# Query weights turned in 32x32 blocks on VectorE and gathered through DRAM, in place of transposing matmuls on TensorE

## The chip, the cores and the metric

The kernel runs on one core of a Trainium2 chip. The metric is the time of one execution on the device in microseconds (us), as the median of several runs. The engines of the core are named as the profile names them: PE is TensorE (PEld its weight loads), DVE is VectorE, ACT is ScalarE, POOL is GpSimd, and SP is SyncE, which issues all DMAs of this kernel.

## The reference

Attention by way of 49 agents, followed by a two-layer network with a squared ReLU, all in float32:

```python
B, N, C = (4, 12480, 128);  n_agents = 49;  d_ff = 2048

def sm(a, b):
    s = scale * (a @ b.transpose(0, 2, 1))
    s = s - s.max(-1, keepdims=True)
    e = np.exp(s)
    return e / (e.sum(-1, keepdims=True) + 1e-09)
a2k = sm(agents, k)            # 49 x N weights a batch
agent_v = a2k @ v              # 49 x 128
q2a = sm(q, agents)            # N x 49 weights: the "query weights"
x = (q2a @ agent_v)            # N x 128
h = np.maximum(x @ w_in, 0.0)
out = h * h @ w_out
```

## The kernel before

**Tiling.** The 49,920 tokens are cut into 52 groups of 960 (`BLK`, 13 groups a batch). A group is 8 tiles of 120 tokens (`TP` = 120, `NT` = 8) and is worked on in two halves of 480 tokens (`G`). The hidden dimension of 2048 is 16 chunks of 128; two chunks of one half make a *slot*, so a group has 16 slots (`SLOTS`), and slots are handled in pairs.

**What the main loop computes.** `w_in` is multiplied beforehand with the agents' values, once a batch (`tables`). A half's hidden values are then one product of its query weights, 49 rows and 480 columns, with that table. To keep float32 accuracy on the faster matmul type both operands are split into a rounded part (`hi`) and a remainder (`lo`), so that the product has three parts: hi with hi, hi with lo and lo with hi. Their rows stand on top of one another along the contraction: 49 rows of hi and 49 of lo, 98 (`K2`), then 30 more rows of hi (`SP` = 128 - 98) in the same tile `w`, and the 19 that are left over (`NL`) in a small tile `x`, which holds four copies of them, at partitions 0, 32, 64 and 96. `first(k)` (L341) issues four matmuls with `w` and four with `x` for a pair of slots; `hidden(k)` (L359) makes relu and square on ACT and DVE, and the split of the square on ACT, DVE and POOL; `second(k)` (L384) issues the 12 matmuls of the output a pair of slots, four slots behind. All of them pass `queued` (L334), so that their instructions bear line L337.

**How the query weights are made.** `queries(g + 1)` (L282) is a generator that advances by one step in slot 0 and in each slot from 2 on of group `g` (L492 to L496). The steps before:

1. load `qt`, the queries as 128 x 960 (L285);
2. 8 score matmuls into the bank `psa`, tokens on partitions (L290; each is two instructions in the trace);
3. maximum and subtraction on DVE (L293, L295);
4. exponential on ACT (L297);
5. sum and reciprocal on DVE (L300 to L302), product on POOL (L303);
6. the rounded half on ACT (L188) into tile `pp`, 98 columns a token;
7. the remainder on POOL (L190);
8. for each half: 4 matmuls with a unit matrix that turn `pp` (98 rows out, L312), a copy from `psa` to `w` on ACT (L317), and in the next step one DMA of the 30 rows (L320) and four of the 19 rows (L322).

The weights of a group must be in `w` and `x` when `first` of its first slot (or of its ninth, for the second half) runs.

**Other work beside it.** While a batch is in its main loop, `background(b + 1)` (L401) works through keys and values of the next batch in small steps: loads `kt` and `vt` (480 KB each, two buffers), score matmuls (L155), sums over the values (L235), the next tables (L266 to L277). It is spread over 88% of a batch's slots, and the last batch has none. `bank()` gives background and queries the same single PSUM bank `psa`; only before the main loop (`alone`) do they take banks of the pool `h`, of which there are three pairs. The hidden values use these three, and `o` is one bank.

**What sets the order.** Instructions are emitted in the order of the Python code; a planner at build time lays out each engine's order by that priority and by when it reckons an instruction's inputs to be ready, so that later emitted work can stand ahead where an engine would be free. On the chip each engine, SP with its DMAs too, goes through its own list in order and waits at the head for what it needs.

The prologue runs the first batch's keys and values (`whole_values`), `queries(0)` and `tables(0)`, and decodes `w_in` and `w_out`.

Of the kernel before, what the change touches and what calls it, by code (L numbers as in the profile page):

```python
# [9 lines left out]
F32 = mybir.dt.float32  # L10
F32R = mybir.dt.float32r
# [6 lines left out]
P = 128  # L18
TP = 120
NT = 8  # L20
BLK = TP * NT
G = BLK // 2
# [15 lines left out]
@with_exitstack  # L38
def agent_attention_relu2(ctx: ExitStack, tc: tile.TileContext, qT, kT, v, agT, w_in, w_out, outT):
    nc = tc.nc  # L40
    C, NTOK = qT.shape
    _, B, NA = agT.shape
    N = NTOK // B
    FF = w_in.shape[1]
    NCH = FF // P
    NB = N // BLK
    NTT = N // TP
    K2 = 2 * NA
    SP = P - K2
    NL = NA - SP  # L50
    NQ = P // 32
    scale = 1.0 / math.sqrt(C)

    const = ctx.enter_context(tc.tile_pool(name="const", bufs=1))
    kv = ctx.enter_context(tc.tile_pool(name="kv", bufs=2))
    sp = ctx.enter_context(tc.tile_pool(name="sp", bufs=NB))
    small = ctx.enter_context(tc.tile_pool(name="small", bufs=1))
    aw = ctx.enter_context(tc.tile_pool(name="aw", bufs=2))
    qp = ctx.enter_context(tc.tile_pool(name="qp", bufs=2))
    dec = ctx.enter_context(tc.tile_pool(name="dec", bufs=2))  # L60
    ps_h = ctx.enter_context(tc.tile_pool(name="ps_h", bufs=3, space=PSUM))
    ps_o = ctx.enter_context(tc.tile_pool(name="ps_o", bufs=1, space=PSUM))
    ps_a = ctx.enter_context(tc.tile_pool(name="ps_a", bufs=1, space=PSUM))

    ag = const.tile([C, B, NA], F32, name="ag")
# [2 lines left out]
    nc.gpsimd.memset(ones, 1.0)  # L68
    ident = const.tile([P, P], F32, name="ident")
    make_identity(nc, ident)  # L70
    identr = const.tile([TP, TP], F32R, name="identr")
    nc.scalar.copy(identr, ident[:TP, :TP])

    quad = const.tile([K2, 2, NA], F32, name="quad")
    nc.gpsimd.tensor_copy(quad, ident[:K2, :K2].rearrange("p (h a) -> p h a", h=2))
# [50 lines left out]
    last = {}  # L126
# [3 lines left out]
    def bank():  # L130
        if alone[0]:
            return ps_h.tile([P, 2, 512], F32, name="h")[:, 0, :]
        return ps_a.tile([P, 512], F32, name="psa")
# [51 lines left out]
    def halves(out, x, n, eng):  # L185

        w = x.shape[2]
        nc.scalar.copy(out[:, :, :w], x)  # L188
        yield
        last[eng] = eng.tensor_sub(out[:, :, n : n + w], x, out[:, :, :w].bitcast(F32))  # L190

    def whole_values(b, i, vt):
        st = state[b]
        e = st["s"][i]
        nc.vector.tensor_sub(e, e, st["mb"].rearrange("p (o a) -> p o a", o=1).broadcast_to([TP, NT, NA]))
        nc.scalar.activation(e, e, AF.Exp, scale=scale)
        if i == 0:
            st["pv"] = bank()
        for t in range(NT):
            nc.tensor.matmul(  # L200
                st["pv"][:NA, :C], e[:, t, :], vt[:, t, :], start=(i == 0 and t == 0), stop=(i == NB - 1 and t == NT - 1)
            )
        if i == 1:
            st["es"] = small.tile([TP, NT, NA], F32, name="es")
        if i > 0:
            nc.gpsimd.tensor_add(st["es"], st["es"] if i > 1 else st["s"][0], e)

# [35 lines left out]
    def tables(b):  # L243
        st = state[b]
        qd = quad.rearrange("p h a -> p (h a)")
        if "x" not in st:
            st["x"] = small.tile([K2, C + 1], F32, name="x")
            nc.vector.tensor_add(st["x"], st["av"][:, : C + 1], st["av"][:, C + 1 :])
        x = st["x"]
        yield  # L250
        pa = bank()
        nc.tensor.matmul(pa[:C, :K2], x[:, :C], qd, start=True, stop=True)
        nc.tensor.matmul(pa[:K2, K2 : K2 + 1], qd, x[:, C:], start=True, stop=True)
        yield
        av = small.tile([C, K2], F32, name="avT")
        nc.scalar.copy(av, pa[:C, :K2])
        rl = small.tile([K2, 1], F32, name="rl")
        nc.vector.tensor_scalar_add(rl, pa[:K2, K2 : K2 + 1], 1e-9)
        nc.vector.reciprocal(rl, rl)
        hi = st["hi"] = aw.tile([P, FF], F32R, name="aw_hi")  # L260
        ex = st["lo"] = aw.tile([P, NCH // NQ, P], F32R, name="aw_ex")
        for n in range(FF // 512):
            yield
            cs = slice(n * 512, (n + 1) * 512)
            pw = bank()
            nc.tensor.matmul(pw[:K2, :], av, win[:, cs], start=True, stop=True)  # L266
            yield
            last[nc.scalar] = nc.scalar.activation(hi[:K2, cs], pw[:K2, :], AF.Copy, scale=rl)
            lo = aw.tile([NA, 512], F32R, name="aw_lo", bufs=3)
            last[nc.vector] = nc.vector.scalar_tensor_tensor(  # L270
                out=lo, in0=pw[:NA, :], scalar=rl[:NA, :], in1=hi[:NA, cs].bitcast(F32),
                op0=ALU.mult, op1=ALU.subtract,
            )
            yield
            nc.sync.dma_start(hi[K2:, cs].bitcast(F32), lo[:SP, :].bitcast(F32))
            for t in range(NQ):
                nc.sync.dma_start(ex[t * 32 : t * 32 + NL, n, :].bitcast(F32), lo[SP:, t * P : (t + 1) * P].bitcast(F32))  # L277


    weights = {}  # L280

    def queries(g):  # L282
        b = g // NB
        qt = qp.tile([C, BLK], F32, name="qt", bufs=1)
        nc.sync.dma_start(qt, qT[:, g * BLK : (g + 1) * BLK])  # L285
        yield
        ps = bank()
        sv = ps[:TP, : NT * NA].rearrange("p (t a) -> p t a", a=NA)
        for t in range(NT):
            nc.tensor.matmul(sv[:, t, :], qt[:, t * TP : (t + 1) * TP], ag[:, b, :], start=True, stop=True)  # L290
        yield
        m = qp.tile([TP, NT, 1], F32, name="m", bufs=1)
        nc.vector.reduce_max(m, sv, axis=AX.X)  # L293
        e = qp.tile([TP, NT, NA], F32, name="e", bufs=1)
        nc.vector.tensor_sub(e, sv, m.broadcast_to([TP, NT, NA]))  # L295
        yield
        nc.scalar.activation(e, e, AF.Exp, scale=scale)  # L297
        yield
        z = qp.tile([TP, NT, 1], F32, name="z", bufs=1)
        nc.vector.reduce_sum(z, e, axis=AX.X)  # L300
        nc.vector.tensor_scalar_add(z, z, 1e-9)  # L301
        nc.vector.reciprocal(z, z)  # L302
        nc.gpsimd.tensor_mul(e, e, z.broadcast_to([TP, NT, NA]))  # L303
        yield
        pp = qp.tile([TP, NT, K2], F32R, name="pp", bufs=1)
        yield from halves(pp, e, NA, nc.gpsimd)
        weights[g] = []
        for j in range(2):
            yield
            pt = bank()  # L310
            for t in range(NT // 2):
                nc.tensor.matmul(  # L312
                    pt[:K2, t * TP : (t + 1) * TP], pp[:, j * (NT // 2) + t, :], identr, start=True, stop=True
                )
            w = qp.tile([P, G], F32R, name=f"w{j}", bufs=2)
            x = qp.tile([P, G], F32R, name=f"x{j}", bufs=2)
            nc.scalar.copy(w[:K2, :], pt[:K2, :G])  # L317
            weights[g].append((w, x))
            yield
            nc.sync.dma_start(w[K2:, :].bitcast(F32), w[:SP, :].bitcast(F32))  # L320
            for t in range(NQ):
                nc.sync.dma_start(x[t * 32 : t * 32 + NL, :].bitcast(F32), w[SP:NA, :].bitcast(F32))  # L322

    NP = NCH // 2
# [74 lines left out]
    def background(b):  # L401

        kt = load_keys(b, 0, kv, "kt")
        for i in range(NB):
            nxt = load_keys(b, i + 1, kv, "kt") if i + 1 < NB else load_values(b, 0, kv, "vt")
            yield from scores(b, i, kt)
            yield
            kt = nxt
        yield from maxima(b)
        yield  # L410
        vt = kt
        for i in range(NB):
            nxt = load_values(b, i + 1, kv, "vt") if i + 1 < NB else None
            yield from values(b, i, vt, nc.gpsimd)
            yield
            vt = nxt
        yield from tables(b)
# [64 lines left out]
    for k in range(total + LAG):  # L482
        if k < total:
            g, c = divmod(k, SLOTS)
            b, i = divmod(g, NB)
            if i == 0 and c == 0 and b + 1 < B:
                todo = background(b + 1)
                done = 0
            goal = (i * SLOTS + c + 1) * STEPS / (SPREAD * NB * SLOTS)
            while done < goal and step(todo):  # L490
                done += 1
            if c == 0 and g + 1 < B * NB:  # L492
                ahead = queries(g + 1)
                step(ahead)
            if c >= 2:
                step(ahead)  # L496
        if k % 2 == 0:
            hs = first(k) if k < total else ()
            if hs:
                hidden(k, hs[0])  # L500
            for n in range(2):
                if k + n >= LAG:
                    second(k + n - LAG)
            copied_out()
            if hs:
                hidden(k + 1, hs[1])
# [31 lines left out]
```

## Time and profile before

| | |
|---|---|
| median of 3 runs | 2060.38 us (2060.13 to 2062.12) |
| the profiled execution: its time | 2060.99 us |
| its span, first to last instruction | 2059.2 us |
| granted TensorE clock, mean | 0.992 |
| busy: PE, ACT, DVE, POOL | 99%, 87%, 82%, 62% |
| DMA: moved, share of 16 engines | 131.36 MB, 21.0% |

The profiled execution is one run on the chip; its rows carry the name of the tile written, an arrow, and the tiles read, with the line of the kernel behind the engine. A busy share is an average over stages. [...] Of a DMA the profile shows its issue on SP; when its data moves is seen in the DMA share and GB/s of short windows.

### The profile page before, as it was taken

How to read it: one execution, taken by the hardware profiler on the slowest of the kernel's cores; microseconds unless marked ns; L12 is line 12 of the kernel's file. 1: busy time of each engine (PE TensorE's matmuls, PEld its weight loads, DVE VectorE, ACT ScalarE, POOL GpSimd, SP SyncE). 2: the span in 40 equal slices, each digit the busy share in tenths (PEclk: the TensorE clock that was granted, in tenths of full speed). 3: DMA queues.
4: the chain of work that ended last, by engine and by line, in shares of the span. 5: the costliest groups of instructions: out<-in, count | busy, mean ns of one | idle time of the engine just before them, and what ended most of it. 6: DMA issues, size and time to landing. Idle time of an engine off the chain costs nothing.

```text
span 2059.2 us, 31857 instructions
## 1 busy us (share of the span) xinstructions
PE 2029.8 (99%) x11014; PEld 1589.8 (77%) x11014; DVE 1686.1 (82%) x1842; ACT 1782.3 (87%) x2100; POOL 1279.2 (62%) x1104
## 2 busy tenths in 40 slices
PE   9799999999999999999999999999999999999999
PEld 8588777777788777777778877777777777777777
DVE  5687888888887888888887788888888888888887
ACT  3478999989888899989888899998889898989897
POOL 3555787765544587776555467877555555656555
PEclk9799999999999999999999999999999999999999
DMA  9532122121122221221112212211111111111100
GB/s 288 160 92 76 59 72 74 53 77 41 45 81 65 62 72 54 72 71 57 55 54 69 68 42 61 74 58 49 42 50 36 45 36 46 37 41 36 38 23 20
DMA packets 55604, 131.36 MB, mean 64 GB/s; under 512 B 6660, under 2 KB 34388, under 8 KB 55444
## 3 DMA queue, kind: packets, MB, share of 16 engines
q1 hardware_dynamic: 55444, 129.33, 21.0%
q8 instruction: 88, 1.44, 0.3%
q14 instruction: 72, 0.59, 0.1%
HBM read 80.97 MB, written 25.56 MB: 52 GB/s over the span
## 4 chain that ended last, share of the span: by engine, by line
PE 53%; DVE 1%; issue 0%; ACT 0%
PE o L337 33%; PE h L337 16%; PE psa L290 2%; PE psa L155 1%; PE psa L312 1%; PE psa L235 1%; PE psa L266 0%; DVE h L337 0%; DVE gg L337 0%; DVE g_lo L337 0%; DVE z L301 0%; ACT r L337 0%; DVE ob L337 0%; ACT g_hi L337 0%; DVE av L241 0%
## 5 line engine op out<-in xcount | busy, mean ns | idle before, releaser
L372 POOL TENSOR_TENSOR g_lo<-gg,g_hi 128x480 fp32r<-128x480 f32 x832 | 999.2, 1222 | 685.7 <-DVE gg L337 489.1
L337 ACT ACTIVATE r<-h 128x960 f32<-128x960 f32 x832 | 800.9, 963 | 150.0 <-PE h L337 141.9
L337 ACT ACTIVATE g_hi<-r 128x960 fp32r<-128x960 f32 x832 | 837.7, 1007 | 34.1 <-POOL e L190 0.7
L337 DVE TENSOR_TENSOR h<-r,h 128x960 f32<-128x960 f32 x416 | 482.4, 1160 | 160.2 <-ACT r L337 157.8
L337 DVE TENSOR_TENSOR gg<-r,h 128x960 f32<-128x960 f32 x416 | 477.8, 1149 | 81.9 <-ACT r L337 81.0
L337 PE MATMUL o<-g_hi,wo_hi 128*128 128x480 f32 x1664 | 543.0, 408 | 0.0
L337 DVE TENSOR_TENSOR g_lo<-h,g_hi 128x960 fp32r<-128x960 f32 x416 | 480.8, 1156 | 45.2 <-ACT g_hi L337 8.1
L337 PE MATMUL o<-g_hi,wo_lo 128*128 128x480 f32 x1664 | 498.7, 381 | 0.0
L337 PE MATMUL o<-g_lo,wo_hi 128*128 128x480 f32 x1664 | 497.7, 380 | 0.0
L337 PE MATMUL h<-w,aw_hi 128*128 128x480 f32 x1664 | 483.3, 398 | 9.7 <-DVE gg L337 8.1
L337 PEld LDWEIGHTS o<-g_hi,wo_hi 128*128 128x128 f32 x1664 | 280.8, 188 | 118.8 <-issue 70.1
L337 PEld LDWEIGHTS o<-g_hi,wo_lo 128*128 128x128 f32 x1664 | 313.4, 188 | 51.3
L337 PEld LDWEIGHTS o<-g_lo,wo_hi 128*128 128x128 f32 x1664 | 313.0, 188 | 50.9
L337 PEld LDWEIGHTS h<-w,aw_hi 128*128 128x128 f32 x1664 | 289.0, 190 | 56.9 <-DVE gg L337 17.5
L337 PE MATMUL h<-x,aw_ex 19*128 19x480 f32 x1664 | 205.4, 481 | 0.1
L337 PEld LDWEIGHTS h<-x,aw_ex 19*128 19x128 f32 x1664 | 80.5, 182 | 140.7 <-issue 139.7
L290 PEld LDWEIGHTS psa<-ag,qt 128*120 128x120 f32 x816 | 102.2, 187 | 7.8 <-issue 1.4
L337 DVE COPY ob<-o 128x480 f32<-128x480 f32 x104 | 68.3, 656 | 39.8 <-PE o L337 38.3
L290 PE MATMUL psa<-ag,qt 128*120 128x49 f32 x816 | 98.1, 264 | 0.0
L190 POOL TENSOR_TENSOR vs<-vt,vs 120x1024 fp32r<-120x1024 f32 x39 | 86.3, 2213 | 16.7 <-ACT vs L188 16.4
L155 PEld LDWEIGHTS psa<-ag,kt 128*120 128x120 f32 x624 | 74.7, 185 | 4.8 <-DVE mx L163 0.6
L155 PE MATMUL psa<-ag,kt 128*120 128x49 f32 x624 | 71.9, 262 | 0.2 <-DVE mx L163 0.2
(109 smaller groups left out, 1026.6 us busy)
## 6 DMA issues: line engine op xcount, KB each, us to landing
qt<-in_qT SPq DMA_DIRECT2D x52, 480.0 KB
out_T<-ob SPq DMA_DIRECT2D x104, 240.0 KB
kt<-in_kT SPq DMA_DIRECT2D x39, 480.0 KB
vt<-in_v SPq DMA_DIRECT2D x39, 480.0 KB
x<-w SPq DMA_DIRECT2D x416, 35.6 KB
ahead<-in_kT SPq DMA_DIRECT2D x13, 480.0 KB
ahead<-in_v SPq DMA_DIRECT2D x13, 480.0 KB
w<-w SPq DMA_DIRECT2D x104, 56.2 KB
```

The source lines that it names most:

```text
L155: nc.tensor.matmul(sv[:, t, :], kt[:, t * TP : (t + 1) * TP], ag[:, b, :], start=True, stop=True)
L190: last[eng] = eng.tensor_sub(out[:, :, n : n + w], x, out[:, :, :w].bitcast(F32))
L235: nc.tensor.matmul(pv[:K2, :W], e[:, t, :], vs[:, t, :], start=(t == 0), stop=(t == NT - 1))
L290: nc.tensor.matmul(sv[:, t, :], qt[:, t * TP : (t + 1) * TP], ag[:, b, :], start=True, stop=True)
L312: nc.tensor.matmul(pt[:K2, t * TP : (t + 1) * TP], pp[:, j * (NT // 2) + t, :], identr, start=True, stop=True)
L337: ins = issue(*args, **kw)
L372: nc.gpsimd.tensor_sub(lo[:, n, :], gg[:, n, :], hi[:, n, :].bitcast(F32))
```

## The change

- The queries are laid out on the host for 128 tokens a tile, of which 120 are real: each quadrant of 32 partitions has 30 tokens and 2 columns of zeros. `qt` grows from 960 to 1024 columns. Score matmuls, maxima, sums and products work on 128 partitions.
- `e` becomes part of a constant tile `qe` of 64 columns a token tile, zero behind the 49 agents. DVE turns it in blocks of 32x32: after that a quadrant's partitions are 32 agents (or the 17 left over, in the second block), and the free dimension is the 30 tokens of that quadrant.
- ACT rounds the turned tile (`et_hi`), POOL takes the remainder (`et_lo`). Both go to a scratch `d` in DRAM, and eight DMAs read them back as rows of `w`: for hi and lo and each half, 32 agents and 17 agents, each row in four pieces of 120 tokens, 480 bytes.
- The matmuls with the unit matrix, their PSUM bank and the copies from it are gone. `w` and `x` hold both halves in one tile, so one DMA fills the 30 rows and four fill the 19, of both halves at once.
- `load_queries` loads the queries of the group after next behind the score matmuls. The generator has one step less for the load and is advanced from slot 1 on.
- To make room, `es` uses the buffers of `mx`, and `aw_lo` has two buffers in place of three.

```diff
-    C, NTOK = qT.shape
+    C, NTOK = outT.shape
+    HT = NT // 2
+    TW = TP // NQ
+    turn = ctx.enter_context(tc.tile_pool(name="turn", bufs=2, space=bass.MemoryType.DRAM))
-    identr = const.tile([TP, TP], F32R, name="identr")
-    nc.scalar.copy(identr, ident[:TP, :TP])
+    qe = const.tile([P, NT, 64], F32, name="qe")
+    nc.gpsimd.memset(qe, 0.0)
...
-            st["es"] = small.tile([TP, NT, NA], F32, name="es")
+            st["es"] = st["mx"]
...
-            lo = aw.tile([NA, 512], F32R, name="aw_lo", bufs=3)
+            lo = aw.tile([NA, 512], F32R, name="aw_lo")
...
+    asked = {}
+
+    def load_queries(g):
+        qt = asked[g] = qp.tile([C, NT, P], F32, name="qt", bufs=1)
+        nc.sync.dma_start(qt, qT[:, g * NT * P : (g + 1) * NT * P])
...
-        qt = qp.tile([C, BLK], F32, name="qt", bufs=1)
-        nc.sync.dma_start(qt, qT[:, g * BLK : (g + 1) * BLK])
-        yield
+        if g == 0:
+            load_queries(g)
+            yield
+        qt = asked.pop(g)
...
-            nc.tensor.matmul(sv[:, t, :], qt[:, t * TP : (t + 1) * TP], ag[:, b, :], start=True, stop=True)
-        yield
+            nc.tensor.matmul(sv[:, t, :], qt[:, t, :], ag[:, b, :], start=True, stop=True)
+        if g + 1 < B * NB:
+            load_queries(g + 1)
+        yield
...
-        pp = qp.tile([TP, NT, K2], F32R, name="pp", bufs=1)
-        yield from halves(pp, e, NA, nc.gpsimd)
-        weights[g] = []
-        for j in range(2):
-            yield
-            pt = bank()
-            for t in range(NT // 2):
-                nc.tensor.matmul(
-                    pt[:K2, t * TP : (t + 1) * TP], pp[:, j * (NT // 2) + t, :], identr, start=True, stop=True
-                )
-            w = qp.tile([P, G], F32R, name=f"w{j}", bufs=2)
-            x = qp.tile([P, G], F32R, name=f"x{j}", bufs=2)
-            nc.scalar.copy(w[:K2, :], pt[:K2, :G])
-            weights[g].append((w, x))
-            yield
-            nc.sync.dma_start(w[K2:, :].bitcast(F32), w[:SP, :].bitcast(F32))
-            for t in range(NQ):
-                nc.sync.dma_start(x[t * 32 : t * 32 + NL, :].bitcast(F32), w[SP:NA, :].bitcast(F32))
+        et = qp.tile([P, 2, NT, 32], F32, name="et", bufs=1)
+        nc.vector.transpose(et.rearrange("p a t i -> p t a i"), qe.rearrange("p t (a i) -> p t a i", i=32))
+        et = et.rearrange("p a t i -> p (a t) i")[:, :, :TW]
+        yield
+        hi = qp.tile([P, 2 * NT, TW], F32R, name="et_hi", bufs=1)
+        nc.scalar.copy(hi, et)
+        yield
+        lo = qp.tile([P, 2 * NT, TW], F32R, name="et_lo", bufs=1)
+        last[nc.gpsimd] = nc.gpsimd.tensor_sub(lo, et, hi.bitcast(F32))
+        flat = []
+        for y in (hi, lo):
+            d = turn.tile([P, 4, HT * TW], F32, name="d")
+            nc.sync.dma_start(d, y.rearrange("p (x t) i -> p x (t i)", t=HT).bitcast(F32))
+            flat.append(d.rearrange("(r a) x n -> a x r n", r=NQ))
+        w = qp.tile([P, 2, G], F32R, name="w", bufs=2)
+        x = qp.tile([P, 2, G], F32R, name="x", bufs=2)
+        yield
+        for n, y in enumerate(flat):
+            for j in range(2):
+                to = w[:, j, :].rearrange("k (r n) -> k r n", r=NQ).bitcast(F32)
+                nc.sync.dma_start(to[n * NA : n * NA + 32], y[:, j, :, :])
+                nc.sync.dma_start(to[n * NA + 32 : (n + 1) * NA], y[: NA - 32, 2 + j, :, :])
+            yield
+        nc.sync.dma_start(w[K2:, :, :].bitcast(F32), w[:SP, :, :].bitcast(F32))
+        for t in range(NQ):
+            nc.sync.dma_start(x[t * 32 : t * 32 + NL, :, :].bitcast(F32), w[SP:NA, :, :].bitcast(F32))
+        weights[g] = [(w[:, j, :], x[:, j, :]) for j in range(2)]
...
-            if c >= 2:
+            if c >= 1:
                 step(ahead)
...
+    turned = np.zeros((B * N // G, NT // 2, 4, 32, C), q.dtype)
+    turned[:, :, :, : TP // 4] = q.reshape(-1, 4, NT // 2, TP // 4, C).transpose(0, 2, 1, 3, 4)
-        "qT": np.ascontiguousarray(q.reshape(B * N, C).T),
+        "qT": np.ascontiguousarray(turned.reshape(-1, C).T),
```

More of the change, by code (lines that the diff above doesn't have):

```diff
@@ L280, in agent_attention_relu2 @@
     weights = {}
+    asked = {}
+    def load_queries(g):
+        qt = asked[g] = qp.tile([C, NT, P], F32, name="qt", bufs=1)
+        nc.sync.dma_start(qt, qT[:, g * NT * P : (g + 1) * NT * P])
     def queries(g):
         b = g // NB
-        qt = qp.tile([C, BLK], F32, name="qt", bufs=1)
-        nc.sync.dma_start(qt, qT[:, g * BLK : (g + 1) * BLK])
-        yield
[L287 to L290, printed above, removed]
-        yield
-        m = qp.tile([TP, NT, 1], F32, name="m", bufs=1)
+        if g == 0:
+            load_queries(g)
+            yield
+        qt = asked.pop(g)
+        ps = bank()
+        sv = ps[:, : NT * NA].rearrange("p (t a) -> p t a", a=NA)
+        for t in range(NT):
+            nc.tensor.matmul(sv[:, t, :], qt[:, t, :], ag[:, b, :], start=True, stop=True)
+        if g + 1 < B * NB:
+            load_queries(g + 1)
+        yield
+        m = qp.tile([P, NT, 1], F32, name="m", bufs=1)
         nc.vector.reduce_max(m, sv, axis=AX.X)
-        e = qp.tile([TP, NT, NA], F32, name="e", bufs=1)
-        nc.vector.tensor_sub(e, sv, m.broadcast_to([TP, NT, NA]))
+        e = qe[:, :, :NA]
+        nc.vector.tensor_sub(e, sv, m.broadcast_to([P, NT, NA]))
         yield
@@ L298, in queries @@
         yield
-        z = qp.tile([TP, NT, 1], F32, name="z", bufs=1)
+        z = qp.tile([P, NT, 1], F32, name="z", bufs=1)
         nc.vector.reduce_sum(z, e, axis=AX.X)
@@ L302, in queries @@
         nc.vector.reciprocal(z, z)
-        nc.gpsimd.tensor_mul(e, e, z.broadcast_to([TP, NT, NA]))
+        nc.gpsimd.tensor_mul(e, e, z.broadcast_to([P, NT, NA]))
         yield
-        pp = qp.tile([TP, NT, K2], F32R, name="pp", bufs=1)
-        yield from halves(pp, e, NA, nc.gpsimd)
-        weights[g] = []
-        for j in range(2):
-            yield
-            pt = bank()
-            for t in range(NT // 2):
-                nc.tensor.matmul(
-                    pt[:K2, t * TP : (t + 1) * TP], pp[:, j * (NT // 2) + t, :], identr, start=True, stop=True
-                )
-            w = qp.tile([P, G], F32R, name=f"w{j}", bufs=2)
-            x = qp.tile([P, G], F32R, name=f"x{j}", bufs=2)
-            nc.scalar.copy(w[:K2, :], pt[:K2, :G])
-            weights[g].append((w, x))
-            yield
-            nc.sync.dma_start(w[K2:, :].bitcast(F32), w[:SP, :].bitcast(F32))
-            for t in range(NQ):
-                nc.sync.dma_start(x[t * 32 : t * 32 + NL, :].bitcast(F32), w[SP:NA, :].bitcast(F32))
+        et = qp.tile([P, 2, NT, 32], F32, name="et", bufs=1)
```

## The prediction

> **What bounds the kernel now.** I read the page's busy times first, then the row of one long window over the main loop, then the chain of waits inside one group of the last batch.
>
> ```profile
> PE 2029.8 (99%) x11014; PEld 1589.8 (77%) x11014; DVE 1686.1 (82%) x1842; ACT 1782.3 (87%) x2100; POOL 1279.2 (62%) x1104
> 150.00:2040.00 1890.00, 1884.96 (x10102) 1466.82 (x10102) 1570.72 (x1660) 1695.49 (x1972) 1205.16 (x1021) 1.00 0.18 55
> ```
>
> The columns after the window are its length, then busy time of PE, PEld, DVE, ACT and POOL, then the granted clock, the DMA share and GB/s. From 150 to 2040 us PE is idle 5 us in 1890, at full clock. A piece of work taken off PE there shortens the kernel by what it took, until something else is late. The chain shows what it took:
>
> ```profile
> 1681.19 2.82 PE o L337 x12
> 1684.00 0.44 PE h L337 x2
> 1684.45 0.32 PE psa L312 x4
> 1684.77 0.90 PE h L337 x5
> 1688.49 0.32 PE psa L312 x4
> 1688.81 1.34 PE h L337 x7
> 1692.98 1.30 PE h L337 x8
> 1701.06 1.36 PE L290 MATMUL psa<-ag,qt 128*120 128x49 f32 x12
> ```
>
> The columns are start, length, what. One pair of slots is 12 output matmuls (2.82 us) and 8 hidden ones (1.30), 4.12 us, eight times a group. The last row, from the timeline, is the next group's scores; the same row one group earlier starts at 1665.69 (quoted below), so a group takes 35.37 us.
>
> **The change part by part.** *The transposing matmuls go.* Each batch of four is 0.32 us of the chain, and the hidden matmuls beside it take 1.34 instead of 1.30. There are 52 groups with two batches: 104 x 0.32 = 33.3 us, or 104 x 0.36 = 37.4 with the disturbance. I take 35 off. The bank that they filled is `psa`, of which there is one.
>
> *The scores load 128 columns instead of 120.* They are 52 x 16 instructions (an f32 matmul is issued as two).
>
> ```profile
> L290 PEld LDWEIGHTS psa<-ag,qt 128*120 128x120 f32 x816 | 102.2, 187 | 7.8 <-issue 1.4
> L337 PEld LDWEIGHTS h<-w,aw_hi 128*128 128x128 f32 x1664 | 289.0, 190 | 56.9 <-DVE gg L337 17.5 <-issue 5.5 <-DVE aw_lo L270 2.0
> 995.63 1.41 PE psa L290 x14
> ```
>
> A load of 128 columns lasts 190 ns against 187, so the rise may be nothing. But in the chain 14 of them take 1.41 us, 0.101 each, and the transposing ones, which load 98 columns, 0.080 each: 0.82 to 0.84 ns a column in both, as if paced by the load. Then 8 columns more cost 0.0067 us each, 832 x 0.0067 = 5.6 us. I take 5 added; bounds 0 and 5.6.
>
> *ScalarE* loses two PSUM copies a group, keeps exp, and its rounding copy grows from 392 to 480 elements.
>
> ```profile
> L337 ACT ACTIVATE g_hi<-r 128x960 fp32r<-128x960 f32 x832 | 837.7, 1007 | 34.1 <-POOL e L190 0.7 <-issue 0.4
> L337 ACT ACTIVATE r<-h 128x960 f32<-128x960 f32 x832 | 800.9, 963 | 150.0 <-PE h L337 141.9
> L317 ACT CAST w<-psa 98x480 fp32r<-98x480 f32 x102 | 55.7, 546 | 2.8 <-PE psa L312 1.6 <-PE h L337 0.3
> L295 DVE TENSOR_TENSOR e<-psa,m 120x392 f32<-120x392 f32 x51 | 28.7, 563 | 1.3
> L337 DVE TENSOR_TENSOR g_lo<-h,g_hi 128x960 fp32r<-128x960 f32 x416 | 480.8, 1156 | 45.2 <-ACT g_hi L337 8.1
> ```
>
> In a group without background work that leaves it 16 x (1.007 + 0.963) + 0.52 + 0.55 = 32.6 us beside PE's 35.37 - 0.70 + 0.1 = 34.8. It stays under PE by some 2 us, so this part is worth nothing directly.
>
> *VectorE* gains a transpose of 512 elements a partition that no row shows. Its bounds are the 392-element row (0.56 us) and the 960-element one (1.16); nearest is the first, and I take 0.7 us. DVE is 82% busy, so 52 x 0.7 = 36 us lie beside PE; were that cover gone, they would be the price. GpSimd's subtraction grows from 392 to 480 elements, at 62% busy: nothing.
>
> *The gather* adds to SP two writes to DRAM of 240 KB and eight reads a group and merges the ten copies into five of twice the size. No row has such a read; SP's issues of today are these:
>
> ```profile
> 1676.48 0.34 SPq L382 DMA_DIRECT2D out_T<-ob  x1
> 1685.60 0.86 SPq L320 DMA_DIRECT2D w<-w  x1
> SPq L382 <- DVE ob L337: 417.3, 78, 16.1
> kt<-in_kT SPq DMA_DIRECT2D x39, 480.0 KB
> vt<-in_v SPq DMA_DIRECT2D x39, 480.0 KB
> 62.00:66.00 4.00, 2.05 (x11) 1.93 (x12) 0.82 (x1) 0.00 (x0) 0.95 (x1) 0.50 1.00 250
> ```
>
> At 0.34 to 0.86 us each, ten cost 3.4 to 8.6 us of 35 on a queue that mostly waits (417 us for ob alone, up to 16 at a time). What the gather puts on the path is latency, weighed below.
>
> *The prologue* does all this once, while the DMA engines are full (share 1.00 at 62 to 66 us, the last row). I add 1 us, bounds 0 and 5: some 0.9 MB more at that row's 250 GB/s are 3.5 us. The smaller aw_lo pool and es in mx's place touch the prologue only; its bounds cover them.
>
> Sum: -35 + 5 + 1 = -29. The profiled execution took 2060.99 us (span 2059.2), 0.6 above the median of 2060.38; I set the sum against the median: **2031 us**. The bounds of these terms give 2060 - 37 = 2023 and 2060 - 33 + 6 + 5 = 2038.
>
> **Do the weights arrive in time?** This decides the sign. The chain before, in one group:
>
> ```profile
> 1665.69 1.36 PE L290 MATMUL psa<-ag,qt 128*120 128x49 f32 x12
> 1671.66 0.52 ACT L297 ACTIVATE e<-e 120x392 f32<-120x392 f32 x1
> 1678.15 0.84 POOL L303 TENSOR_TENSOR e<-e,z 120x392 f32<-120x392 f32 x1
> 1679.87 0.51 ACT L188 CAST pp<-e 120x392 fp32r<-120x392 f32 x1
> 1682.38 0.98 POOL L190 TENSOR_TENSOR pp<-e,pp 120x392 fp32r<-120x392 f32 x1
> 1667.94 0.35 SPq L285 DMA_DIRECT2D qt<-in_qT  x1
> 1698.18 0.54 ACT L317 CAST w<-psa 98x480 fp32r<-98x480 f32 x1
> 1686.56 2.48 SPq L322 DMA_DIRECT2D x<-w  x4
> x<-w SPq DMA_DIRECT2D x416, 35.6 KB
> 1687.50:1694.00 6.50, 6.50 (x37) 4.94 (x35) 4.91 (x6) 5.81 (x7) 3.81 (x4) 1.00 0.06 21
> 507.47 2.46 SPq L277 DMA_DIRECT2D aw_ex<-aw_lo  x4
> 510.00:511.00 1.00, 1.00 (x6) 0.86 (x5) 1.00 (x1) 0.97 (x2) 0.31 (x1) 1.00 0.06 16
> 1677.00:1678.00 1.00, 1.00 (x9) 0.88 (x6) 0.90 (x2) 0.90 (x1) 1.00 (x2) 1.00 0.63 246
> ```
>
> The rows are timeline rows of PE, ACT, POOL and SP, the x issues of the page, and three windows. The four x copies (19 rows each) run at a DMA share of 0.06, one sixteenth: a single DMA engine, at 21 GB/s. A group's eight make 8 x 35.6 KB = 292 thousand bytes; all of it must now be there before the group's first slot, 13.9 us on that engine, where half had to be before. Ahead of them stand the reads. Those of 17 partitions make 17 x 4 = 68 pieces of 480 B; four of them, 272. If they too go to one engine, the nearest row is aw_ex's 512 B rows, 16 GB/s, 32 ns each: 8.7 us. The other end is a whole 1920 B row at 21 GB/s, 91 ns: 25 us.
>
> [...]
>
> Forecast's case: the query work runs ahead. qt is issued 33 us before its use (1667.94, against 1701.06), and the scores start at 1701.06 as soon as the copy at 1698.18 has emptied the psa bank and PE finishes its next batch; so the bank held them back, not the order in the code. Without the transposes' use of it they can go up to a group earlier. Then only the slot of w holds the reads; the group before last leaves it when 12 output matmuls (2.82 us) still stand before the next group: read issue and start 3 us (eight of 0.34 and some delay), packets 8.7, landing 1, w and the first x 1.9, x 13.9 make 28.5 us, where 34.8 + 0.9 + 2.8 = 38.5 are to be had. It holds up to 68 ns a packet.
>
> **The rivals.** *Weights late (slower).* If the scores keep their lead, 1.4 us ahead of the group as now plus the two slots (4.1) that the code moves them up, 5.5 + 34.8 + 0.9 = 41.2 us are to be had. The chain takes 14.7 to the end of hi (1665.69 to 1680.38), 1.0 for the transpose, 2.5 for the write (out's issue at 1676.48, traffic to 1678, landing), 2 to issue the hi reads, 8.7 for packets (the lo reads stand before x on the engine), 1 landing, 1.9, and x 13.9: 45.7, less an estimated 2.5, since w and x need only the hi half and lo's packets move meanwhile: 43.2. Late by 2 us a group, PE stalls at each start: 51 x 2 = 102, **2133 us**. It decides from a chain over 41 us; at 91 ns a packet the lateness would be 18 us and the time near 2950. For it: the DMA chain is three hops longer. Against it: today's steps start soon after they are ready, hi 0.9 us after the product (1678.99 to 1679.87) and lo 2.0 after hi.
>
> *SP stands in the way.* Waiting for d to land, SP holds up kt, vt and out behind it. The 39 kt and 39 vt loads late by 0.5 us each would cost 39 us: **2070 us**. Against: SP's waits of today, as long as they are, leave PE idle 5 us.
>
> *ScalarE and the hidden banks take over.* With ACT at 32.6 of 34.8 us, bunched work can leave PE waiting for h, and the change does not save what it says. Half of the gain gone: **2046 us**. Against: ACT loses 1.06 us a group (two copies of 0.546, against 0.51 grown to 0.55), PE only 0.6.
>
> **How the numbers follow.** Forecast 2031: 0.55. Weights late: 0.24. SP in the way: 0.12, half of it within the noise of no change. ScalarE takes over: 0.09. A measurement of this kernel tells about 0.2% (4 us) from no change: faster 0.55 + 0.09 = 0.64, same 0.06, slower 0.30. The forecast's own range is 2023 to 2038. For eight in ten it reaches to the SP rival and to the price of late weights; left out are about 0.16 of late weights beyond it and 0.03 below 2020: 2020 to 2135.
>
> **What would show it.** Right: no L312 rows; PE still busy in 99%; the last batch's group at 34.6 to 34.8 us; L290's mean pace in the chain 0.107; its start many slots before its group. Wrong: PEld or PE rows of h that wait for a DMA into x or w at each group's start (late weights), for kt or at L155 (SP), or longer waits of h for DVE's gg and ACT's r (ScalarE). A transpose over 1.2 us, or reads over 68 ns a packet, would break the sum.

## The result, and the profile after

The changed kernel is slower: **2256.19 us**, the median of 4 runs (2255.62 to 2262.81), against 2061.25 (2060.13 to 2063.64) for the kernel before, measured beside it. The ratio is 1.0951, with a 95% interval of 1.0928 to 1.0974. Forecast were 2031 us, with a range of 2020 to 2135.

From the page of the changed kernel: busy times, then three rows of the span in 40 slices (busy tenths of PE, its granted clock, the DMA share).

```profile
span 2254.3 us, 31133 instructions
PE 2072.8 (92%) x10598; PEld 1619.0 (72%) x10598; DVE 1725.9 (77%) x1894; ACT 1752.0 (78%) x1995; POOL 1287.7 (57%) x1105
...
PE   8588988999887889988999988889999999999999
...
PEclk9689988999988899998999988889999999999999
DMA  9523344223343233243211113321111111111110
```

PE was idle 2059.2 - 2029.8 = 29 us before and is idle 2254.3 - 2072.8 = 181 us now: 152 of the 195 us more. The other 43 are in the busy time itself: 416 instructions fewer are busy for longer, since the clock sinks where PE has stood still (mean 0.936, against 0.992). The rows of slices show where: in the first two thirds, where the DMA share is high. The last quarter is all nines.

The same window over the main loop, of the kernel before and then of the changed one, with a later window below. The columns are those of the window rows in the prediction.

```profile
150.00:1400.00 1250.00, 1245.75 (x6795) 974.65 (x6795) 1025.80 (x1101) 1115.67 (x1321) 824.34 (x696) 1.00 0.22 64
```

```profile
150.00:1400.00 1250.00, 1126.11 (x5830) 884.76 (x5829) 923.71 (x1046) 932.50 (x1098) 739.07 (x624) 0.92 0.30 88
...
1628.00:1900.00 272.00, 272.00 (x1323) 205.97 (x1322) 232.79 (x215) 254.32 (x265) 159.05 (x133) 1.00 0.13 40
```

In 1250 us PE is now idle 124 us where it was idle 4, and *no* engine is busier than before: DVE, ACT and POOL have lost too. That is what waiting for something outside the engines looks like. After 1628 us PE doesn't stand still at all (272.00 of 272.00). What is different there? The next view is the window row of the score matmuls alone (L290 before, L299 after; 16 instructions a group):

```profile
150.00:613.00 463.00, 22.76 (x192) 1.00 0.22 64
```

```profile
150.00:613.00 463.00, 38.54 (x272) 0.93 0.35 102
613.00:1121.00 508.00, 43.29 (x304) 0.91 0.33 96
1121.00:1628.00 507.00, 34.16 (x224) 0.94 0.19 61
1628.00:2254.00 626.00, 0.00 (x0) 1.00 0.12 38
```

With 48 instructions ahead of 150 us, the kernel before has done the scores of (48 + 192) / 16 = 15 groups at 613 us, while its main loop has done the products with `w` of 13.4 groups (428 of them, 32 a group). The changed kernel, with 32 ahead of 150 us, has done the scores of 19 groups, while its main loop has done 10.4 (334). After 1628 us there are none left to do: **the query work has run ahead**. In the order of PE's instructions the scores stood 0.7 to 2 groups ahead of the main loop before; now those of group 6 stand 2.5 groups ahead, those of group 12 5.9, of 24 11.7 and of 51 21.6. The planner moves each step to where it reckons PE to be free, and nothing stops it any more: before, the bank that the transposing matmuls filled was copied into `w0` and `w1`, two buffers deep, so that neither this bank nor the scores that need it next could run further. The changed kernel parks its turned weights in the scratch in DRAM, and only the reads into `w` wait for a buffer. The scratch holds nothing back: at 1584 us the writes of all 52 groups have been issued and the reads of 33, although its pool asks for two buffers; why these don't bind, no run shows. That it was the transposes that bound the lead is read from the code; the runs below show what a bound is worth.

Who waits for what, rows chosen from the waits of the changed kernel (engine, tile, line, what ended the wait; us in all, times, longest):

```profile
ACT vs L191 <- DMA vt<-in_v: 53.9, 7, 15.9
PE psa L299 <- DMA qt<-in_qT: 48.8, 7, 10.2
...
ACT et_hi L321 <- DMA d<-et_hi: 42.8, 5, 9.5
...
PE h L356 <- DVE gg L356: 40.8, 12, 13.6
...
DVE aw_lo L273 <- DMA aw_ex<-aw_lo: 28.9, 3, 12.7
...
PE psa L158 <- DMA kt<-in_kT: 21.5, 5, 6.0
PE psa L299 <- DVE aw_lo L273: 21.3, 2, 10.7
...
PE h L356 <- DMA aw_ex<-aw_lo: 10.8, 1, 10.8
...
PEld h L356 <- DMA w<-d: 6.4, 19, 0.3
```

Apart from the last row they are few and long: the longest of each row took 6 to 16 us. Most name a transfer (the longest wait for gg is traced to one below), and these are *transfers of other things*: the weights themselves are late by 6.4 us in the whole run, never by more than 0.3. One such stall, from the timeline of SP, ACT, DVE and PE, in order of time:

```profile
709.14 2.47 SPq L341 DMA_DIRECT2D x<-w  x4
711.71 0.36 SPq L328 DMA_DIRECT2D d<-et_hi  x1
712.18 0.37 SPq L150 DMA_DIRECT2D vt<-in_v  x1
712.64 1.16 SPq L328 DMA_DIRECT2D d<-et_lo  x1
...
726.97 1.99 ACT L191 CAST vs<-vt 120x1024 fp32r<-120x1024 f32 x2 [15.95 <-DMA vt<-in_v]
...
729.93 1.16 DVE L356 TENSOR_TENSOR gg<-r,h 128x960 f32<-128x960 f32 x1 [16.48 <-ACT r L356]
...
731.14 1.17 PE L356 MATMUL h<-w,aw_hi 128*128 128x480 f32 x2 [13.62 <-DVE gg L356]
```

Two windows of the same stretch:

```profile
713.00:716.00 3.00, 3.00 (x17) 2.61 (x16) 0.42 (x2) 0.00 (x0) 0.00 (x0) 1.00 0.93 234
717.00:727.00 10.00, 0.52 (x5) 0.40 (x4) 0.00 (x0) 0.03 (x1) 0.00 (x0) 0.59 0.07 27
```

The four `x` copies are issued at 709.14, `vt` half a microsecond behind them, and it lands 15 us later. Until 716 nearly all DMA engines work (share 0.93). Then for ten microseconds the share is 0.07, one engine of sixteen, at 27 GB/s, and everything else stands still. The four copies of 71.2 KB are 292 thousand bytes, 10.8 us at that rate: the other engines have finished their parts of `vt`, and its last part stands behind `x` on this one. The packets of the trace, counted by size, show it: of the 120 rows of `vt`, 4096 bytes each, 112 have started by 717 us; from 718 to 724 nothing starts but rows of 3840 bytes, those of `x`, six or seven a microsecond, and two single words of 4 bytes; and the last eight of `vt` start between 725 and 727. ACT waits for it in its order, DVE for ACT, PE for DVE. SP had issued all of it by 713.80; its own queue isn't what holds.

The share of 0.07 and the order of the packets make of these 19-row copies a plug for the part of `vt` on their engine. PE loses more than the wait: its last matmul ends at 717.52, the granted clock is 1.00 until 718.78 and 0.50 from there on (0.59 over the ten microseconds), and it is whole again only at 735.84, 4.7 us after PE's next matmul starts.

### The profile page after: what moved, and what is told of

Its sections match the earlier page's. It is cut to its first block, busy times and chain, and to the rows that moved or that the text cites. A ratio compares the mean times of both kernels' runs of the same rounds, so it can differ in the third digit from the quotient of the medians.

```text
span 2254.3 us, 31133 instructions
## 1 busy us (share of the span) xinstructions
PE 2072.8 (92%) x10598; PEld 1619.0 (72%) x10598; DVE 1725.9 (77%) x1894; ACT 1752.0 (78%) x1995; POOL 1287.7 (57%) x1105
## 5 line engine op out<-in xcount | busy, mean ns | idle before, releaser
L356 PE MATMUL o<-g_hi,wo_hi 128*128 128x480 f32 x1664 | 555.6, 416 | 0.0
L356 PE MATMUL h<-w,aw_hi 128*128 128x480 f32 x1664 | 473.9, 397 | 63.2 <-DVE gg L356 40.8
L356 PE MATMUL o<-g_lo,wo_hi 128*128 128x480 f32 x1664 | 513.1, 389 | 0.0
L356 PE MATMUL o<-g_hi,wo_lo 128*128 128x480 f32 x1664 | 510.9, 389 | 0.0
L356 PEld LDWEIGHTS h<-w,aw_hi 128*128 128x128 f32 x1664 | 308.2, 193 | 118.8 <-DVE gg L356 46.9
L356 PEld LDWEIGHTS o<-g_hi,wo_hi 128*128 128x128 f32 x1664 | 288.9, 193 | 120.8 <-ACT g_hi L356 56.4
L356 PEld LDWEIGHTS o<-g_hi,wo_lo 128*128 128x128 f32 x1664 | 321.5, 193 | 53.3
L299 PE MATMUL psa<-ag,qt 128*128 128x49 f32 x816 | 119.5, 303 | 71.9 <-DMA qt<-in_qT 48.8
L299 PEld LDWEIGHTS psa<-ag,qt 128*128 128x128 f32 x816 | 121.7, 225 | 80.8 <-issue 32.0
L158 PE MATMUL psa<-ag,kt 128*120 128x49 f32 x624 | 81.6, 284 | 24.5 <-DMA kt<-in_kT 21.5
## 6 DMA issues: line engine op xcount, KB each, us to landing
x<-w SPq DMA_DIRECT2D x208, 71.2 KB
```

The lines of the kernel that those rows point to most:

```text
L158: nc.tensor.matmul(sv[:, t, :], kt[:, t * TP : (t + 1) * TP], ag[:, b, :], start=True, stop=True)
L299: nc.tensor.matmul(sv[:, t, :], qt[:, t, :], ag[:, b, :], start=True, stop=True)
L356: ins = issue(*args, **kw)
```

## The experiments

Four theories. **A**, the transfers: the 19-row copies, now all of a group's in one burst on one DMA engine, delay the loads behind them. **B**, the order: the query work runs ahead without a bound and crowds into the first two thirds. **C**, formed when the first runs left a kernel as fast as before and no faster: 16 scores in one block crowd PE against ACT and DVE. **D**, formed last: run-ahead loses time only while the lead grows. The ratios below are to the kernel before on the same chip (2061.5 to 2061.8 us), with their 95% intervals.

**Copies of 32 rows.** 13 more rows that no matmul reads come along, and more DMA engines work: behind one such set the DMA share is 0.53 over four microseconds (372 to 376 us), where it was 0.07.

```diff
-            nc.sync.dma_start(x[t * 32 : t * 32 + NL, :, :].bitcast(F32), w[SP:NA, :, :].bitcast(F32))
+            nc.sync.dma_start(x[t * 32 : (t + 1) * 32, :, :].bitcast(F32), w[SP : SP + 32, :, :].bitcast(F32))
```

> The four copies into x take 32 rows instead of 19, nothing else. Theory A (the x copies of both halves, 292 KB on one DMA engine, hold up the part of each kt, vt and qt load that goes through that engine by 10 to 12 us, and PE, ACT and SP, each in its fixed order, wait for these loads): with 32 rows the copies move at a DMA share far over 0.06, the waits of PE for qt and kt (70 us) and of ACT for vt (54 us) nearly go, and the time falls from 2256 to between 2020 and 2080. Theory B (the planner puts the score matmuls up to 18 groups ahead of their use, and PE waits there for queries that were loaded too late whatever the DMA engine does): the waits for qt stay near 50 us and the time above 2180.

2101.33 us, ratio 1.0194 (1.0172 to 1.0216). The waits of this run:

```profile
ACT vs L191 <- DMA vt<-in_v: 20.9, 6, 7.6
...
PE psa L299 <- DMA qt<-in_qT: 10.4, 5, 4.2
```

155 us come back by moving *more* bytes. The long waits shrink to less than half, but 40 us stay, and the time is over the range that A gave: A is a large part, not all.

**Query steps kept in their slot.** The planner may not set a step of `queries` ahead of the last PE instruction emitted before it; the scores then stand 1.0 group ahead.

```diff
             if c == 0 and g + 1 < B * NB:
                 ahead = queries(g + 1)
-                step(ahead)
-            if c >= 1:
+            with tc.issue_after(chain[nc.tensor]) if nc.tensor in chain else ExitStack():
                 step(ahead)
```

> Each step of the queries is kept behind the matmul that was emitted before it on PE, so that the scores can't run ahead of their slot; the copies into x stay as they are. Theory A: kt and vt still stand behind the x copies on one DMA engine; the waits for kt and vt stay, the time stays above 2130, and weights that are now late may add to it. Theory B: the waits for qt go and the time falls below 2100.

2125.63 us, ratio 1.0308 (1.0293 to 1.0323), between the two forecasts. So the edit for B alone is worth 131 us. No wait for `qt` is left; waits of PE for `kt` (24.4 us) and `aw_ex` (11.3) are.

**Both edits.**

> Both edits. Theory A: as with the wide copies alone, 2020 to 2080, unless the pinned chain brings the weights late. Theory B: below 2080 and as with the pin alone.

2061.42 us, ratio 1.000 (0.999 to 1.0009). The whole loss is gone. But so is the forecast gain. The chain of waits in a group of the last batch, where no background work runs (a quiet group from here on):

```profile
1698.60 1.72 PE psa L299 x16
...
1705.87 0.96 ACT r L356
...
1706.86 1.02 ACT g_hi L356
...
1707.89 1.15 DVE gg L356
1709.03 0.63 DVE et L317
...
1709.72 0.58 ACT et_hi L321
...
1734.00 1.72 PE psa L299 x16
```

From one block of scores to the next it is 35.40 us, as long as before (35.37), though the transposes are gone. Behind the block of scores the chain leaves PE for ACT and DVE: their work for the hidden values and for the queries comes due together.

**The copies in two sets of half the size, a step apart.** Narrow as in the changed kernel, no bound.

```diff
-            nc.sync.dma_start(x[t * 32 : t * 32 + NL, :, :].bitcast(F32), w[SP:NA, :, :].bitcast(F32))
+            nc.sync.dma_start(x[t * 32 : t * 32 + NL, 0, :].bitcast(F32), w[SP:NA, 0, :].bitcast(F32))
+        yield
+        for t in range(NQ):
+            nc.sync.dma_start(x[t * 32 : t * 32 + NL, 1, :].bitcast(F32), w[SP:NA, 1, :].bitcast(F32))
```

> The x copies of 19 rows are issued in two sets of four, one for each half, one step apart, as the kernel before did: the same bytes on the same DMA engine in two bursts of 6 us instead of one of 12. Theory A: a load stands behind one burst at most where the second isn't issued yet, the waits for loads shrink by a third to a half, 2130 to 2200. Theory B: no change within 1%, 2235 to 2280.

2243.08 us, ratio 1.0874 (1.0858 to 1.0891). Only 13 us, in the range of B, and the waits for `vt` (71.3 us) and `qt` (63.6) are longer than the changed kernel's. But the run didn't test what it was made for, as SP's timeline shows:

```profile
645.09 2.47 SPq L341 DMA_DIRECT2D x<-w  x4
647.60 2.92 SPq L344 DMA_DIRECT2D x<-w  x4
```

The second set is issued 0.04 us behind the first, in all groups but two: on the chip it is still one burst, since nothing keeps the steps apart. So this run decides nothing between A and B.

**Scores in two blocks, and in four** (with 32 rows and the steps in their slot; two blocks shown, `% 2` for four).

```diff
             nc.tensor.matmul(sv[:, t, :], qt[:, t, :], ag[:, b, :], start=True, stop=True)
+            if g and t + 1 < NT and (t + 1) % 4 == 0:
+                yield
```

> Wide copies and pin, and the scores of a group in two blocks of four tiles in two slots. In the pinned kernel a quiet group takes 35.40 us where 34.7 were counted: after the 1.72 us block of scores ScalarE stands idle for 1.96 us, and the query steps then crowd behind it with the hidden work. Theory C (this crowding costs the 0.7 us): the idle time of ScalarE halves, the quiet group falls to 34.7 to 35.0 us, the time to 2025 to 2045. If what is missing is elsewhere: 2055 to 2065.

2073.54 us, ratio 1.0053 (1.0036 to 1.007), over both forecasts. The quiet group falls to 34.75 us (its scores start at 1758.41 and 1793.16), as C says, but the batches with background work lose more than that gains: at group 30 the run is 23.9 us behind the one with a single block (1309.36 against 1285.50).

> The same with four blocks of two tiles in four slots, so that the weights come three slots later. Theory C: the quiet group 34.6 to 34.8 us and the time 2025 to 2040, if the weights are still in time; if not, a wait for x at each group's start and a time above 2061.

2259.59 us, ratio 1.0955 (1.0923 to 1.0988), as slow as the changed kernel and for another reason. Its waits:

```profile
PE h L358 <- DMA x<-w: 39.0, 38, 2.8
...
PE h L358 <- DMA w<-w: 20.4, 10, 5.2
PE h L358 <- DMA w<-d: 19.0, 14, 2.2
```

And its chain of waits at one group's start:

```profile
1930.22 0.66 DVE ob L358
...
1931.96 0.53 SPq L403
...
1933.38 4.68 DMA w<-d
...
1938.11 0.52 SPq L343
...
1939.95 2.35 DMA x<-w
...
1942.35 0.48 PE h L358
```

Here the weights are late: PE waits for them in 37 of the 52 groups. SP stands at the store of `out_T` (L403) until `ob` is there, the reads from the scratch queue behind it, and then come landing, issues and copies, one after the other. With three more steps before the gather and no freedom to run ahead, there is no slack left.

**The kernel before with the burst.** To it alone are added four narrow copies behind each set, into a tile `y` that nothing reads (and the smaller buffers of the changed kernel, to make room).

```diff
+            y = qp.tile([P, G], F32R, name="y", bufs=2)
+            for t in range(NQ):
+                nc.sync.dma_start(y[t * 32 : t * 32 + NL, :].bitcast(F32), w[SP:NA, :].bitcast(F32))
```

> The kernel before, with four more copies of the same 19 rows into a tile that nothing reads, behind the four into x, so that each half sends 292 KB through one DMA engine where it sent 146; aw_lo and es as in the changed kernel, to make room. Theory A: that engine is now busy some 28 us of a group's 37 with copies, the parts of kt, vt and qt that go through it are late by up to 14 us, and the time rises by 60 to 300 us, with waits of PE and ACT for kt, vt or qt. If single-engine copies don't hold up loads: 2055 to 2070.

2126.37 us, ratio 1.031 (1.0295 to 1.0326). From its waits:

```profile
PE psa L155 <- DMA kt<-in_kT: 20.6, 3, 10.2
...
ACT vs L188 <- DMA vt<-in_v: 19.5, 2, 9.9
```

With nothing of the new gather in it, the old kernel gets the same kind of stall, 10 us behind a burst of eight narrow copies. The mechanism of A belongs to the copies and needs nothing of the change.

**The kernel before with 32-row copies.**

> The kernel before with 32 rows in the copies into x. Theory A: it had 5 us of idle PE in its main loop, so there is nothing to win: 2055 to 2064. If the copies on one engine cost the kernel before something too: below 2050.

2061.65 us, ratio 1.000 (0.999 to 1.0009). The old bursts of half the size harmed nothing; the widening is no improvement in its own right.

**A lead with a bound.** The steps of a slot may run ahead, but not past PE's work of 16 slots (one group) earlier; the scores then stand at most 2.0 groups ahead, as in the kernel before.

```diff
+    marks = []
...
-                step(ahead)
-            if c >= 1:
+            marks.append(chain.get(nc.tensor))
+            with tc.issue_after(marks[k - 16]) if k >= 16 and marks[k - 16] else ExitStack():
                 step(ahead)
```

> Wide copies, and each query step kept behind the matmul that stood 16 slots (one group) earlier, so that the scores run at most one group ahead of the code, as far as they ran in the kernel before. If only the unbounded run-ahead harms and a bounded one helps the planner to fill gaps: below 2050 and below the kernel before. If the query steps crowd wherever they stand: 2055 to 2070 as with the pin.

With 32-row copies: **2048.79 us**, ratio 0.9933 (0.9921 to 0.9946), faster than the kernel before. The long window:

```profile
150.00:1400.00 1250.00, 1241.62 (x6592) 962.23 (x6591) 1064.75 (x1143) 1101.79 (x1269) 842.06 (x706) 1.00 0.33 93
```

PE is idle 8 us of 1250 at full clock, with the same gather and a higher DMA share (0.33) than the changed kernel has (0.30).

> The same with a lead of 8 slots, half a group. Between the pinned kernel (2061) and the lead of 16, or the better of the two by a few us, since the scores then fall into the middle of a group.

Eight slots: 2051.31 us, ratio 0.9949 (0.9935 to 0.9962). The exact bound matters little.

> The lead of 16 slots with the narrow copies of 19 rows on one DMA engine. Theory A: loads still stand behind 12 us of copies; above 2110, like the pinned kernel with narrow copies (2126), and 50 to 80 us over the same lead with wide copies. If the run-ahead alone were the cause: within 15 us of the wide one.

16 slots with the *narrow* copies: 2081.81 us, ratio 1.0098 (1.0085 to 1.0111). So the four corners are:

| | copies of 19 rows | copies of 32 rows |
|---|---|---|
| no bound on the lead | 2256 (the changed kernel) | 2101 |
| bound of 16 slots | 2082 | 2049 |

Each edit alone takes off 155 or 174 us, both 207: the two causes raise each other's price. Narrow copies cost 155 us where the work runs ahead without a bound and 33 under this one, less than the 50 to 80 that A had forecast, and the time is below its 2110. With the steps kept in their slot they cost 64 (2125.63 against 2061.42), though nothing runs ahead there: their price doesn't hang on the lead alone.

**The bound with the scores in two blocks** (32 rows).

> Wide copies, the lead of 16 slots, and the scores in two blocks of four tiles. A quiet group took 35.4 us with the lead and the block of eight, as in the kernel before. Theory C (the block of scores starves ScalarE, and the steps behind it crowd): a quiet group at 34.7 to 34.9 us, and with a lead that leaves the weights a group of time, 2035 to 2046. If the second block delays the background work as it did in the pinned kernel, which took 12 us more with two blocks: 2049 to 2062.

**2042.93 us**, ratio 0.9908 (0.9891 to 0.9924), the fastest. Its chain in the last batch is PE from end to end:

```profile
1896.85 0.82 PE psa L299 x8
...
1901.83 0.82 PE psa L299 x8
...
1931.68 0.82 PE psa L299 x8
```

A group takes 1931.68 - 1896.85 = 34.83 us (34.73 in the two before it), where one block took 35.40.

**Wider bounds, with the narrow copies:** 32 slots, and 128.

> Narrow copies, a lead of at most two groups; the scores reach it at about group 9 of 52. Theory D (it loses only while the lead grows): some 10 us a group up to group 9, as the changed kernel does there, and then nothing more against the lead of one group: 2135 to 2170, and no wait of PE for qt after group 10. Theory E (a lead costs by itself, in every group that has it): a loss that goes on to the end of the third batch, small at this lead, 2085 to 2120.

2091.92 us, ratio 1.0149 (1.0127 to 1.0172).

> The same with at most eight groups, which the scores reach at about group 19 or 20. Theory D: as the changed kernel up to there, some 200 us behind the lead of one group, then level, with little won back at the end: 2240 to 2285. Theory E: a loss in proportion, and still growing in groups 20 to 38: 2120 to 2230 by its end.

2141.62 us, ratio 1.039 (1.0371 to 1.041). Both times lie in the ranges of E, and below those of D by 43 and 98 us; the course of the loss has to decide. To see when the time is lost, take the start of each group's copy-out on DVE (`ob<-o`) from the timelines, all four with narrow copies but the first with the old kernel's, and subtract:

```
group  before  16 slots  32 slots  128 slots  no bound   128 - 16   no bound - 16
  2     207.7     241.7     239.9      240.8     241.6       -0.9         -0.1
  4     283.3     320.0     334.0      343.4     342.7       23.5         22.7
 10     512.4     542.0     556.5      640.4     639.1       98.4         97.1
 14     670.7     703.4     719.7      793.6     856.5       90.2        153.1
 18     823.4     852.9     868.7      944.4    1048.6       91.5        195.8
 30    1286.7    1312.9    1327.7     1399.7    1546.2       86.8        233.3
 50    2008.8    2028.0    2039.3     2088.1    2204.4       60.0        176.4
```

The kernel with 128 slots keeps step with the unbounded one to group 10, losing some 12 us a group, (97.1 - 22.7) / 6. Its bound binds when the main loop is in group 11, and from there it loses nothing more; with 32 slots that point is reached at group 4, 14 us behind. The unbounded one goes on to lose until its scores are nearly done, and then wins some back: its last groups need no scores and take 32.9 us. That course is D's: by E the loss of the kernel with 128 slots would still have grown in groups 20 to 38, and it doesn't. Why a growing lead costs time, no run shows. The total came out smaller than I had expected of D, because I had put the points where the bounds bind too late: I took the number of the group whose scores are made for the one in the main loop.

The first row holds the rest of the narrow copies' price under a bound: 241.7 against 207.7 before, and against 213.0 with 32-row copies. 29 of the 33 us are lost by group 2.

## Why the prediction was wrong, step by step

**The terms of the sum held, each by itself.** The matmuls with the unit matrix are gone. Two rows of the changed kernel's chain in the last batch, eight pairs of slots apart:

```profile
1683.09 2.82 PE o L356 x12
...
1715.99 2.81 PE o L356 x12
```

A group without scores takes 32.9 us. With the 1.72 of a block of scores it is 34.6, where the forecast had 34.6 to 34.8. The scores' pace is 1.72 / 16 = 0.1075 us, forecast 0.107. The transpose:

```profile
L317 DVE STREAM_TRANSPOSE et<-qe 128x512 f32<-128x512 f32 x52 | 36.7, 706 | 3.1 <-POOL qe L314 3.1
```

0.706 us, taken at 0.7. The prologue was just over its upper bound where nothing else disturbs it: the run with 32-row copies and the bound of 16 slots is 213.0 - 207.7 = 5.3 us behind at group 2, where I had taken 1 and bounded it by 5. The changed kernel itself is 241.6 - 207.7 = 33.9 us behind there.

**The step that failed is "the query work runs ahead".** I wrote that without the transposes' use of the bank the scores "can go up to a group earlier", and counted this as pure gain for the weights. Two things were wrong. First, I read the chain row of the scores at a group's start as the next group's, 1.4 us ahead of it, when they belonged to a later one: the counts of L290 by window, which I had not looked at, give 15 groups at 613 us. The slack that I feared for was there already. Second, I took the bank for the only thing that the transposes held, and `w`'s two buffers for a bound on what is left. They bound the reads. Scores, exponentials, writes to the scratch and the loads of `qt` had no bound any more, and the lead grew to 21.6 groups. A bound of one group, put back by hand, takes off 174 us.

**The second error is the price of the narrow copies.** I had computed 13.9 us on one DMA engine, from the row with share 0.06, and used it only for the weights' own arrival. That the same engine carries a part of the loads issued behind them did not enter; with 32-row copies, 155 us come back. The rival "SP stands in the way" named the right victims, with 0.5 us a load, 39 us in all; the place was wrong (the queue of a DMA engine, where SP's was free) and the size of a wait was up to 15.9 us. Since its price came from SP's short issues, the rival's end lay at 2070.

**The other rivals.** Weights late, the one I gave most to, isn't what happened (6.4 us); it is what the run with four blocks of scores shows, with the SP queue in its chain. That the reads of 17 rows go to one DMA engine, 8.7 us of packets in my account of the gather, was my assumption, and no run shows it for these reads alone. Between 1690 and 1691 us of the changed kernel 45 pieces of 480 bytes start, with six words of 4 bytes and nothing else, at a share of 0.08, one engine of sixteen: 22 ns a piece where I had taken 32. Nor does a run show the 1 us for landing by itself. ScalarE and the hidden banks: right as a mechanism in the quiet groups, 35.40 - 34.83 = 0.6 us each where the scores come in one block. That the same crowding takes the gain of the 32-row kernel with its steps in their slot in the groups with background work too isn't shown: two blocks made these groups slower.

**What stays open.** The best version gains 18.6 us of the 29 forecast. By group 30 it is level with the kernel before (1285.9 against 1286.7), having made up the 5 us that it started behind, so nearly all of its net gain is in the last 22 groups; why the groups with background work do not gain their 0.6 us each wasn't settled. Nor was it tried whether the loads would escape the plug on a second queue.

## What to carry to other kernels

An operation that is removed may have been a bound: ask which buffer it filled, what could not run further because of it, and put the bound back by hand if a planner would otherwise hoist the work. Small transfers on one DMA engine, here four copies of 19 rows (share 0.07 for ten microseconds), held up a large one issued behind them, and copies of 32 rows took 155 us off; count bytes per DMA engine, not per transfer, and try the wider copy even if the rows added are waste. When all engines lose busy time at once and the waits are few and long, look at the DMA share in the middle of one of them.

## What the runs showed of the hardware that was not expected

- Four copies of 19 rows hold one DMA engine for ten microseconds at 27 GB/s (share 0.07), and a 480 KB load issued 0.5 us behind them landed 15 us later. The same copies with 32 rows move 68% more bytes, and the kernel is 155 us faster without a bound and 33 with one.
- The granted clock fell to half 1.3 us after PE's last matmul in such a stall, came back 4.7 us after PE went on, and was 0.92 as a mean over 1250 us: of the 195 us lost, 43 are in the busy time of PE.
- Issues on SP differ in length: 0.29 us for a read of 17 rows (`w<-d`, L337) and 1.44 for the copy of 30 rows (`w<-w`, L339), in the timeline of the changed kernel. Shape alone doesn't set it: four reads of 32 rows (L336) in the same stretch, 702 to 707 us, took 0.34, 0.39, 2.05 and 1.23.
